# Attention with a gated MLP on one core: other costs for VectorE's queued side work, and none of it handed out in the last block of the MLP's first product

## The chip, the core and the metric

The kernel runs on one core of a Trainium2 chip. Its time is the device time of the whole program in microseconds (us). TensorE (PE in the profile) does the matmuls, VectorE (DVE) and ScalarE (ACT) the elementwise work, GpSimd (POOL) and SyncE (SP) issue DMA transfers from queues of their own. Each engine takes its instructions strictly in the order in which the program lists them.

## The reference

For x of 2048 rows by 1024 columns (bf16):

```
xn  = layernorm(x)
q, k, v = xn @ wqkv             (32 heads of 32 columns)
logits  = q . k[s - 2w], w = 0..7      (a window of 8, dilation 2; masked before row 0)
s   = (softmax(logits * scale) . v[s - 2w]) @ wo
g   = silu( (silu(xn @ w1) * (xn @ w3)) @ w2 )     (inner width 3584)
out = x + s * g
```

## The kernel before

The 2048 rows are worked in four chunks (0 to 3) of 512, one after the other. In each chunk TensorE runs, without a pause if it can:

- the projection to q, k and v (`qkv`, line 254): three times eight groups of eight matmuls of 128x128 by 128x512;
- the MLP's first product (`up_block`): 14 blocks (`fb` = 0 to 13), in each two pairs of groups, `g` from w1 and `u` from w3 (tile `gu`). ScalarE takes silu of `g` into `sg` (line 258), VectorE multiplies that by `u` into one of 28 tiles `ht` (line 260). That makes one `ht` per 16 matmuls;
- the MLP's second product (`down_half`, line 466), twice seven weight tiles, for the two halves of the columns. Each half has four accumulators `acc` in PSUM. All PSUM tiles of `gu` and `acc` come from one pool of six banks, so an accumulator waits until the last reader of its bank's tile before (an `sg` or an `ht`) is through;
- the output projection (`wo_proj`, line 421), in the middle of the second half, or in chunk 3 between the first half and the last (line 489).

The attention itself is done by VectorE beside this, as *side work*. An object `Side` holds a queue of items, each with a cost in us, a function that emits its instructions, and sometimes a gate, a time before which it may not go. `Side` has a clock of its own, counted at build time: after each piece of TensorE's work the program calls `side.step(dt, used)`. The clock goes on by `dt`; a credit grows by `dt − used`, up to 4.0; items are emitted from the head of the queue while the credit is positive, and each takes its cost off. So the costs decide at build time behind which `ht` an item stands on VectorE. They don't alter what an item does. A block of the first product steps twice by 2 * GRP, GRP being 1.727, with 0.7 used for the `ht`.

The items of a chunk, in order:

- eight Q·K windows: a product of 128x4096 (line 311), folds of 2048 and 1024 (line 322) and 512 (line 326) into `E`;
- `shuffle_out`: sixteen DMAs on POOL's queue move `E` to `L4` (line 342); the four loads of the next chunk's x (line 211) go to SP's queue;
- statistics and normalization of the next chunk (lines 199, 222, 231, 202; gate 12 us behind the shuffle; not in chunk 3). Four transposing DMAs on SP's queue (line 235) follow, one at the end of a block (`bring_one`), at the earliest 3 us of side clock after their `norm`;
- the softmax (gate 16 us behind the shuffle): three adds of `L4` into `z` (lines 364 to 366), maximum (369), subtraction (371), exp on ScalarE (358), sum (373), reciprocal (375), product `pb` (376). Silu, exp and the square root of line 225 each need a table load on ScalarE when the function changes;
- `shuffle_back`: sixteen DMAs on POOL's queue move `pb` to `Pr` (line 384);
- eight P·V products of 128x4096 (line 395, gate 16 us behind that shuffle) and seven joins (line 406) into `oT`, in the order product 0, product 1, join; then three times product, product, join, join.

`wo_proj` first flushes what is left in the queue; its matmuls read `oT`. SP's queue also carries the weight loads (line 136), two at a time in the second half of a block, and `load_wo` (line 193) after block 10. A weight load waits until TensorE is through with the tile whose place it takes.

Of the kernel before, what the change touches and what calls it, by code (L numbers as in the profile page):

```python
# [16 lines left out]
class Side:  # L17
# [7 lines left out]
    def add(self, cost, fn, gate=None):  # L25
        self.items.append((cost, fn, gate))

    def step(self, dt, used=0.0):
        self.now += dt
        self.credit = min(self.credit + dt - used, 4.0)  # L30
        while self.items and self.credit > 0:
            cost, fn, gate = self.items[0]
            if gate is not None and gate() > self.now:
                break
            self.items.popleft()
            fn()
            self.credit -= cost
# [8 lines left out]
def kernel(  # L46
# [11 lines left out]
    nc = tc.nc  # L58
    P = 128
    S, D, F = 2048, 1024, 3584  # L60
    Dh, W, DIL = 32, 8, 2
# [5 lines left out]
    FB = FT // 2  # L67
# [4 lines left out]
    GRP = 1.727  # L72
# [27 lines left out]
    side = Side()  # L100
# [53 lines left out]
    def load_x0(st):  # L154
# [15 lines left out]
        out=ident[:], in_=ident[:], compare_op=ALU.not_equal, fill=1.0,  # L170
# [9 lines left out]
        out=maskb[:], in_=maskb[:], compare_op=ALU.is_ge, fill=-1.0e9,  # L180
# [17 lines left out]
    def half_stats(x_t, stats, i):  # L198
        nc.vector.bn_stats(out=stats[:, i, :], in_=x_t[:, i * 512:(i + 1) * 512])  # L199

    def normalize(x_t, mean, rstd):
        nc.vector.tensor_scalar(
            out=x_t[:], in0=x_t[:], scalar1=mean, scalar2=rstd, op0=ALU.subtract, op1=ALU.mult,
        )

    def ln_side(c):
        xs = []
        for st in range(NST):
            x_t = xp.tile([P, D], BF16, tag="x")
            g = (c * NST + st) * P  # L210
            nc.sync.dma_start(out=x_t[:], in_=x_flat[g:g + P, :])
            xs.append(x_t)
        mv = small.tile([P, NST, nc.vector.BN_AGGR_DIM], FP32, tag="mv", bufs=2)
        rstd = small.tile([P, NST], FP32, tag="rstd", bufs=2)
        ready = side.now + 12.0
        mark = [0.0]

        def stat(st):
            stats = small.tile([P, 2, nc.vector.BN_STATS_DIM], FP32, tag="stats")
            half_stats(xs[st], stats, 0)  # L220
            half_stats(xs[st], stats, 1)
            nc.vector.bn_aggr(out=mv[:, st, :], in_=stats[:])

        def root():
            nc.scalar.activation(out=rstd[:], in_=mv[:, :, 1], func=ACTF.Sqrt, bias=eps_t[:], scale=1.0)
            mark[0] = side.now + 2.0

        for st in range(NST):
            side.add(1.45, lambda st=st: stat(st), lambda: ready)
        side.add(0.0, root)  # L230
        side.add(0.15, lambda: nc.vector.reciprocal(out=rstd[:], in_=rstd[:]), lambda: mark[0])
        nxt = xnT_pool.tile([P, KT, CH], BF16, tag="xnT", name="xnT_next")

        def bring(st):
            nc.sync.dma_start_transpose(out=nxt[:, :, st * P:(st + 1) * P], in_=xs[st][:])

        def norm(st):
            normalize(xs[st], mv[:, st, 0:1], rstd[:, st:st + 1])
            brings.append((side.now + 3.0, lambda: bring(st)))

        for st in range(NST):
            side.add(0.55, lambda st=st: norm(st))
        return nxt

    brings = deque()
# [17 lines left out]
    def up_block(c, xnT, fb):  # L263
        hts = []
        w1t, w3t = take_w(("1", fb)), take_w(("3", fb))
        for i in range(2):
            pss = []
            for wt in (w1t, w3t):
                ps = psum_mm.tile([P, CH], FP32, tag="mm", name=f"gu{c}_{fb}_{len(pss)}")
                mm_group(ps[:], lambda kt: wt[:, kt, i * P:(i + 1) * P], lambda kt: xnT[:, kt, :])  # L270
                pss.append(ps)
            if i == 1:
                load_w(2)
            hts.append(gate_up(*pss))
            side.step(2 * GRP, 0.7)
        bring_one()
        return hts

# [25 lines left out]
    att = {}  # L304

    def qk_side(c):
        E = block("E").rearrange("p (w s) -> p w s", w=W)

        def mul(w, prod):
            o = HALO - DIL * w  # L310
            nc.vector.tensor_mul(prod, qT[:], kT[:, :, o:o + CH])  # L311

        def one(w):
            hold = {}

            def first():
                hold["p"] = block("prod").rearrange("p (j s) -> p j s", j=NJ)
                mul(w, hold["p"])

            def fold(n):  # L320
                prod = hold["p"]
                nc.vector.tensor_add(prod[:, 0:n, :], prod[:, 0:n, :], prod[:, n:2 * n, :])  # L322

            def last():
                prod = hold["p"]
                nc.vector.tensor_add(E[:, w, :], prod[:, 0, :], prod[:, 1, :])  # L326

            side.add(2.2, first)
            side.add(1.15, lambda: fold(4))
            side.add(0.6, lambda: fold(2))  # L330
            side.add(0.35, last)

        for w in range(W):
            one(w)
        side.add(0.0, lambda: shuffle_out(c, E))
# [14 lines left out]
    def softmax_side(c, L4):  # L350
        z = sm.tile([P, W, P], FP32, tag="z")
        mx = sm.tile([P, P], FP32, tag="mx")
        ssum = mx
        pb = sm.tile([P, W, P], BF16, tag="pb")
        mark = [0.0]

        def expo():
            nc.scalar.activation(out=z[:], in_=z[:], func=ACTF.Exp, scale=scale)
            mark[0] = side.now + 3.4

        def mask():
            nc.vector.tensor_add(z[0:32, :, 0:HALO], z[0:32, :, 0:HALO], maskb[:])

        side.add(1.2, lambda: nc.vector.tensor_add(z[:], L4[:, 0], L4[:, 1]), lambda: att["L4_at"])
        side.add(1.2, lambda: nc.vector.tensor_add(z[:], z[:], L4[:, 2]))
        side.add(1.2, lambda: nc.vector.tensor_add(z[:], z[:], L4[:, 3]))
        if c == 0:
            side.add(0.3, mask)
        side.add(1.9, lambda: nc.vector.tensor_reduce(
            out=mx[:], in_=z[:].rearrange("p w s -> p s w"), axis=AX.X, op=ALU.max))  # L370
        side.add(1.2, lambda: nc.vector.tensor_sub(z[:], z[:], mx[:].unsqueeze(1).to_broadcast([P, W, P])))
        side.add(0.0, expo)
        side.add(1.9, lambda: nc.vector.tensor_reduce(
            out=ssum[:], in_=z[:].rearrange("p w s -> p s w"), axis=AX.X, op=ALU.add), lambda: mark[0])
        side.add(0.95, lambda: nc.vector.reciprocal(out=ssum[:], in_=ssum[:]))
        side.add(1.2, lambda: nc.vector.tensor_mul(pb[:], z[:], ssum[:].unsqueeze(1).to_broadcast([P, W, P])))  # L376
        side.add(0.0, lambda: shuffle_back(c, pb))

    def shuffle_back(c, pb):
# [9 lines left out]
    def pv_side(c, Pr, ready):  # L389
        oT = block("oT").rearrange("p (j s) -> p j s", j=NJ)  # L390
        att["oT"] = oT

        def pvmul(dst, w):
            o = HALO - DIL * w
            nc.vector.tensor_mul(  # L395
                dst, Pr[:, w, :].unsqueeze(1).to_broadcast([P, NJ, CH]), vT[:, :, o:o + CH]
            )

        hold = {}

        def part(key, w):
            hold[key] = block("pv").rearrange("p (j s) -> p j s", j=NJ)
            pvmul(hold[key], w)

        def join(a, b):
            nc.vector.tensor_add(a, a, b)  # L406

        side.add(2.2, lambda: pvmul(oT, 0), lambda: ready)
        side.add(2.2, lambda: part("B", 1))
        side.add(2.2, lambda: join(oT, hold["B"]))  # L410
        for w0 in (2, 4, 6):
            side.add(2.2, lambda w0=w0: part("B", w0))
            side.add(2.2, lambda w0=w0: part("C", w0 + 1))
            side.add(2.2, lambda: join(hold["B"], hold["C"]))
            side.add(2.2, lambda: join(oT, hold["B"]))

    def wo_piece(oT, was, st, c0, w):
        dh, n0 = divmod(c0, CH)
# [31 lines left out]
    def finish_half(c, dh, gts, s_sb, xres, queue):  # L450
        def one(st):
            finish(c, st, dh * 512, 512, gts[st][:], s_sb[:, st, dh * 512:(dh + 1) * 512], xres, queue)
        for st in range(NST):
            side.add(1.38, lambda st=st: one(st))

    def down_half(c, dh, hts, at):
        accs = [psum_mm.tile([P, 512], FP32, tag="mm", name=f"acc{c}_{dh}_{st}") for st in range(NST)]
# [104 lines left out]
    def copy_in(src, st, ks, eng):  # L562
# [28 lines left out]
        out=junk[:], in_=x0[1][:], func=ACTF.Square, bias=nm[:], scale=1.0 / 32.0, accum_out=mv0[1][:, 1:2],  # L591
# [17 lines left out]
    def part(kt, js, h):  # L609
        cs = slice(h * 256, (h + 1) * 256)  # L610
        for j in js:
            nc.tensor.matmul(  # L612
                qps[j][:, cs], lhsT=wq(kt, j), rhs=xcT[:, kt, cs],
                start=(kt == 0 and h == 0), stop=(kt == KT - 1), skip_group_check=True,
            )
# [106 lines left out]
```

## Time and profile before

| | |
|---|---|
| median of the runs | 821.23 us (820.35 to 821.45, 3 runs) |
| the profiled execution's own time | 820.01 us |
| its span, first to last instruction | 818.2 us |
| TensorE busy | 805.8 us (98%) |
| VectorE busy | 477.1 us (58%) |
| ScalarE busy | 181.5 us (22%) |
| POOL busy | 92.6 us (11%) |

In a row of the time line the first two numbers are the start and the length in us; then follow engine, line, operation, the tiles written and read and their shapes, how many of them are merged in the row, and in square brackets the engine's idle time ahead of it and what ended that. A row of the waits has the engine, tile and line that waited, what it waited for, and then the us in total, how often, and the longest. SPq and POOLq are the sequencers that issue DMAs. A DMA row without a start time names the transfer, its queue, the count and the median us from issue to landing. PE's ends are modelled, and a few per cent of its records are missing, so counts of matmuls in a row can be a few short.

### The profile page before, as it was taken

What the parts mean: (1) busy time and instruction counts of PE and PEld (TensorE: products, weight loads), DVE (VectorE), ACT (ScalarE), POOL (GpSimd) and SP (SyncE); (2) the same over time, 40 slices, a digit from 0 to 9 for tenths busy, and PEclk for the clock granted to TensorE, in tenths of its full rate; (3) what the DMA queues carried; (4) which work ended last, traced back from release to release, by engine and by line L of the source; (5) the groups of instructions that cost most, each with busy time, mean ns of one, the idle gap of its engine ahead of it and who ended that gap; (6) DMA issues with size and microseconds to landing.
All of it is one profiled execution on the core that took longest, in us unless ns stands there. A gap on an engine that the chain in (4) does not pass through costs nothing.

```text
span 818.2 us, 9453 instructions
## 1 busy us (share of the span) xinstructions
PE 805.8 (98%) x3742; PEld 406.8 (50%) x3816; DVE 477.1 (58%) x492; ACT 181.5 (22%) x293; POOL 92.6 (11%) x175
## 2 busy tenths in 40 slices
PE   9999999999999999999999999999999999999998
PEld 7654444444665444444466444444446644444443
DVE  6498564942239775792125958479311694639632
ACT  3031331012332133101133213210123311311120
POOL 0001321001100214000010031400000004030010
PEclk9999999999999999999999999999999999999999
DMA  9676999842366899964244799995434488687500
GB/s 299 185 196 199 206 189 275 255 152 78 109 199 164 222 194 224 277 222 144 76 161 118 205 216 205 203 301 186 138 94 150 110 210 186 165 242 221 179 31 22
DMA packets 195148, 147.44 MB, mean 180 GB/s; under 512 B 23584, under 2 KB 175904, under 8 KB 195104
## 3 DMA queue, kind: packets, MB, share of 16 engines
q1 hardware_dynamic: 189664, 134.76, 60.8%
q0 software_dynamic: 5440, 12.07, 6.7%
q8 instruction: 30, 0.49, 0.3%
q14 instruction: 14, 0.11, 0.1%
HBM read 130.02 MB, written 4.19 MB: 164 GB/s over the span
## 4 chain that ended last, share of the span: by engine, by line
PE 86%; DVE 7%; DMA 3%; issue 2%; POOL 1%; ACT 1%; DVEq 0%; ACTq 0%
PE gu L254 35%; PE acc L466 20%; PE ps_qkv L254 19%; PE ps_wo L421 7%; DMA Pr<-pb 3%; PE acc L489 3%; DVE pv L395 2%; PE ps_qkv L612 1%; POOL Pr L384 1%; DVE ht L260 1%; DVE oT L406 1%; DVE stats L199 1%; DVE pv L406 1%; ACT L258 0%; PE warm_ps L507 0%
## 5 line engine op out<-in xcount | busy, mean ns | idle before, releaser
L254 PE MATMUL gu<-xnT_next,w 128*128 128x512 bf16 x1317 | 289.5, 379 | 1.7 <-ACT sg L258 0.3
L254 PEld LDWEIGHTS <-w 128*128 128x128 bf16 x1792 | 175.3, 98 | 211.9 <-issue 0.9
L466 PE MATMUL acc<-w,ht 128*128 128x512 bf16 x767 | 169.6, 379 | 3.1 <-DVE ht L260 2.3
L254 PEld LDWEIGHTS <-wq 128*128 128x128 bf16 x720 | 103.2, 143 | 52.1
L260 DVE TENSOR_TENSOR ht<-sg,gu 128x512 bf16<-128x512 bf16 x112 | 75.9, 682 | 86.3 <-PE gu L254 65.1
L254 PE MATMUL ps_qkv<-xnT_next,wq 128*128 128x512 bf16 x565 | 124.2, 379 | 0.6
L466 PEld LDWEIGHTS <-ht 128*128 128x128 bf16 x784 | 76.6, 98 | 95.1 <-issue 2.9
L258 ACT ACTIVATE sg<-gu 128x512 bf16<-128x512 f32 x112 | 65.8, 597 | 261.4 <-PE gu L254 221.3
L311 DVE TENSOR_TENSOR prod<-qT,kT 128x4096 bf16<-128x4096 bf16 x32 | 73.1, 2286 | 68.5 <-ACT kT L282 68.5
L254 PE MATMUL gu<-xnT,w 128*128 128x512 bf16 x439 | 96.4, 379 | 0.5
L446 DVE TENSOR_TENSOR gt<-gt,s_sb 128x512 f32<-128x512 f32 x31 | 21.4, 690 | 122.2 <-ACT gt L440 68.5
L342 POOL DMA_DIRECT2D L<-E x64 | 37.1, 586 | 276.4 <-DVE E L326 264.1
L395 DVE TENSOR_TENSOR pv<-Pr,vT 128x4096 bf16<-128x4096 bf16 x28 | 63.3, 2287 | 0.0
L322 DVE TENSOR_TENSOR prod<-prod 128x2048 bf16<-128x2048 bf16 x64 | 61.2, 956 | 1.4
L421 PE MATMUL ps_wo<-wo,oT 128*128 128x512 bf16 (+2 forms) x260 | 55.9, 372 | 0.3
L440 ACT ACTIVATE gt<-acc 128x512 f32<-128x512 f32 x32 | 19.1, 597 | 149.6 <-PE acc L466 127.8
L448 POOL DMA_DIRECT2D out_dram<-o_t x28 | 15.3, 546 | 309.2 <-DVE o_t L447 309.2
L384 POOL DMA_DIRECT2D Pr<-pb x64 | 36.7, 579 | 108.1 <-DVE pb L376 98.0
L421 PEld LDWEIGHTS <-oT 128*128 128x128 bf16 x264 | 25.6, 98 | 30.0
L406 DVE TENSOR_TENSOR oT<-oT,pv 128x4096 bf16<-128x4096 bf16 x16 | 36.6, 2289 | 0.2
L433 ACT CAST s_sb<-ps_wo 128x512 bf16<-128x512 f32 x31 | 18.1, 585 | 66.4 <-PE ps_wo L421 66.4
L282 ACT CAST vT<-ps_qkv 128x512 bf16<-128x512 f32 x32 | 18.7, 585 | 59.7 <-PE ps_qkv L254 58.6
(81 smaller groups left out, 329.0 us busy)
## 6 DMA issues: line engine op xcount, KB each, us to landing
w<-in_B_w_dram SPq DMA_DIRECT2D x168, 512.0 KB, 5.4
wq<-in_A_wqkv_dram SPq DMA_DIRECT2D x44, 512.0 KB, 3.8
wo<-in_A_wo_dram SPq DMA_DIRECT2D x8, 1024.0 KB, 11.2
L<-E POOLq DMA_DIRECT2D x64, 64.0 KB, 7.0
Pr<-pb POOLq DMA_DIRECT2D x64, 64.0 KB, 5.4
xres<-in_A_x_dram SPq DMA_DIRECT2D x4, 1024.0 KB, 6.5
out_dram<-o_t POOLq DMA_DIRECT2D x28, 128.0 KB, 2.0
x_t<-in_A_x_dram SPq DMA_DIRECT2D x12, 256.0 KB, 6.2
```

Of the source, the lines that this page charges most:

```text
L254: nc.tensor.matmul(ps, lhsT=lhs(kt), rhs=rhs(kt), start=(kt == 0), stop=(kt == KT - 1))
L258: nc.scalar.activation(out=sg[:], in_=g_ps[:], func=ACTF.Silu)
L260: nc.vector.tensor_mul(ht[:], sg[:], u_ps[:])
L311: nc.vector.tensor_mul(prod, qT[:], kT[:, :, o:o + CH])
L322: nc.vector.tensor_add(prod[:, 0:n, :], prod[:, 0:n, :], prod[:, n:2 * n, :])
L342: nc.gpsimd.dma_start(out=L4[sq * NH:(sq + 1) * NH, r, :, :], in_=E_r[r, :, :, sq * P:(sq + 1) * P],)
L384: nc.gpsimd.dma_start(out=Pr_r[r, :, :, sq * P:(sq + 1) * P], in_=pb[sq * NH:(sq + 1) * NH, :, :],)
L395: nc.vector.tensor_mul(dst, Pr[:, w, :].unsqueeze(1).to_broadcast([P, NJ, CH]), vT[:, :, o:o + CH])
L406: nc.vector.tensor_add(a, a, b)
L421: nc.tensor.matmul(ps[:, 0:w], lhsT=oT[:, j, st * P:(st + 1) * P], rhs=was[dh][:, j, n0:n0 + w], start=(j == 0), stop=(j == NJ - 1),)
L466: nc.tensor.matmul(accs[st][:], lhsT=hts[f][:, st * P:(st + 1) * P], rhs=w2t[:, i, :], start=(f == 0), stop=(f == FT - 1),)
L489: nc.tensor.matmul(acc[:], lhsT=hts[f][:, st * P:(st + 1) * P], rhs=w2ts[f // 4][:, f % 4, :], start=(f == 0), stop=(f == FT - 1),)
```

## The change

`step` gets an argument `hold`: with it the clock and the credit go on, but no item is emitted. `up_block` sets it in the last of the 14 blocks and counts 0.72 for the `ht`. All costs of side items are set to other numbers. The functions that are emitted are the same.

```diff
-    def step(self, dt, used=0.0):
+    def step(self, dt, used=0.0, hold=False):
...
-        while self.items and self.credit > 0:
+        while not hold and self.items and self.credit > 0:
...
-            side.add(1.45, lambda st=st: stat(st), lambda: ready)
+            side.add(1.6, lambda st=st: stat(st), lambda: ready)
...
-        side.add(0.15, lambda: nc.vector.reciprocal(out=rstd[:], in_=rstd[:]), lambda: mark[0])
+        side.add(0.19, lambda: nc.vector.reciprocal(out=rstd[:], in_=rstd[:]), lambda: mark[0])
...
-            side.add(0.55, lambda st=st: norm(st))
+            side.add(0.57, lambda st=st: norm(st))
...
-            side.step(2 * GRP, 0.7)
+            side.step(2 * GRP, 0.72, hold=fb == FB - 1)
...
-            side.add(2.2, first)
-            side.add(1.15, lambda: fold(4))
-            side.add(0.6, lambda: fold(2))
-            side.add(0.35, last)
+            side.add(2.31, first)
+            side.add(1.25, lambda: fold(4))
+            side.add(0.71, lambda: fold(2))
+            side.add(0.45, last)
```

In the softmax 1.2 becomes 1.24 (three adds, subtraction, product `pb`), 1.9 becomes 1.93 (maximum, sum), 0.95 becomes 0.97 (reciprocal). All fifteen P·V products and joins go from 2.2 to 2.31, and the four last steps of a half's output (`finish_half`) from 1.38 to 1.44.

More of the change, by code (lines that the diff above doesn't have):

```diff
@@ L362, in mask @@
             nc.vector.tensor_add(z[0:32, :, 0:HALO], z[0:32, :, 0:HALO], maskb[:])
-        side.add(1.2, lambda: nc.vector.tensor_add(z[:], L4[:, 0], L4[:, 1]), lambda: att["L4_at"])
-        side.add(1.2, lambda: nc.vector.tensor_add(z[:], z[:], L4[:, 2]))
-        side.add(1.2, lambda: nc.vector.tensor_add(z[:], z[:], L4[:, 3]))
+        side.add(1.24, lambda: nc.vector.tensor_add(z[:], L4[:, 0], L4[:, 1]), lambda: att["L4_at"])
+        side.add(1.24, lambda: nc.vector.tensor_add(z[:], z[:], L4[:, 2]))
+        side.add(1.24, lambda: nc.vector.tensor_add(z[:], z[:], L4[:, 3]))
         if c == 0:
             side.add(0.3, mask)
-        side.add(1.9, lambda: nc.vector.tensor_reduce(
+        side.add(1.93, lambda: nc.vector.tensor_reduce(
             out=mx[:], in_=z[:].rearrange("p w s -> p s w"), axis=AX.X, op=ALU.max))
-        side.add(1.2, lambda: nc.vector.tensor_sub(z[:], z[:], mx[:].unsqueeze(1).to_broadcast([P, W, P])))
+        side.add(1.24, lambda: nc.vector.tensor_sub(z[:], z[:], mx[:].unsqueeze(1).to_broadcast([P, W, P])))
         side.add(0.0, expo)
-        side.add(1.9, lambda: nc.vector.tensor_reduce(
+        side.add(1.93, lambda: nc.vector.tensor_reduce(
             out=ssum[:], in_=z[:].rearrange("p w s -> p s w"), axis=AX.X, op=ALU.add), lambda: mark[0])
-        side.add(0.95, lambda: nc.vector.reciprocal(out=ssum[:], in_=ssum[:]))
-        side.add(1.2, lambda: nc.vector.tensor_mul(pb[:], z[:], ssum[:].unsqueeze(1).to_broadcast([P, W, P])))
+        side.add(0.97, lambda: nc.vector.reciprocal(out=ssum[:], in_=ssum[:]))
+        side.add(1.24, lambda: nc.vector.tensor_mul(pb[:], z[:], ssum[:].unsqueeze(1).to_broadcast([P, W, P])))
         side.add(0.0, lambda: shuffle_back(c, pb))
@@ L406, in join @@
             nc.vector.tensor_add(a, a, b)
-        side.add(2.2, lambda: pvmul(oT, 0), lambda: ready)
-        side.add(2.2, lambda: part("B", 1))
-        side.add(2.2, lambda: join(oT, hold["B"]))
+        side.add(2.31, lambda: pvmul(oT, 0), lambda: ready)
+        side.add(2.31, lambda: part("B", 1))
+        side.add(2.31, lambda: join(oT, hold["B"]))
         for w0 in (2, 4, 6):
[L412 to L415, printed above, removed]
+            side.add(2.31, lambda w0=w0: part("B", w0))
+            side.add(2.31, lambda w0=w0: part("C", w0 + 1))
+            side.add(2.31, lambda: join(hold["B"], hold["C"]))
+            side.add(2.31, lambda: join(oT, hold["B"]))
     def wo_piece(oT, was, st, c0, w):
@@ L453, in finish_half @@
         for st in range(NST):
-            side.add(1.38, lambda st=st: one(st))
+            side.add(1.44, lambda st=st: one(st))
     def down_half(c, dh, hts, at):
```

## The prediction

> **What bounds the kernel now.** I read the page first, then the waits by engine, then the time line around each of TensorE's waits. TensorE is busy for 98% of the span, so the change can only move the time through the gaps in TensorE's row.
>
> ```profile
> PE 805.8 (98%) x3742; PEld 406.8 (50%) x3816; DVE 477.1 (58%) x492; ACT 181.5 (22%) x293; POOL 92.6 (11%) x175
> PE acc L466 <- DVE ht L260: 2.3, 3, 1.1
> PE gu L254 <- ACT sg L258: 0.3, 1, 0.3
> ```
>
> Apart from the start (the warm-up and the first transposes, which the change doesn't touch), TensorE waits four times: three times for an `ht` of VectorE, 2.3 us, once for an `sg` of ScalarE, 0.3 us. The time line puts them at three places:
>
> ```profile
> 548.71 0.81 PE L466 MATMUL acc<-w,ht 128*128 128x512 bf16 x3
> 549.78 1.89 PE L466 MATMUL acc<-w,ht 128*128 128x512 bf16 x8 [0.27 <-DVE ht L260]
> 552.59 32.10 PE L466 MATMUL acc<-w,ht 128*128 128x512 bf16 x145 [0.91 <-DVE ht L260]
> ...
> 750.70 2.75 PE L466 MATMUL acc<-w,ht 128*128 128x512 bf16 x12
> 754.56 21.74 PE L466 MATMUL acc<-w,ht 128*128 128x512 bf16 x98 [1.11 <-DVE ht L260]
> ...
> 709.26 7.07 PE L254 MATMUL gu<-xnT_next,w 128*128 128x512 bf16 x31 [0.25 <-ACT sg L258]
> ```
>
> Two lie where the MLP's second product begins, in chunk 2 (1.18 us) and chunk 3 (1.11 us). What VectorE did there in chunk 2:
>
> ```profile
> 528.06 0.69 DVE L260 TENSOR_TENSOR ht<-sg,gu 128x512 bf16<-128x512 bf16 x1 [2.76 <-remote]
> 536.84 2.29 DVE L395 TENSOR_TENSOR oT<-Pr,vT 128x4096 bf16<-128x4096 bf16 x1 [8.09 <-DMA Pr<-pb]
> 539.05 2.29 DVE L395 TENSOR_TENSOR pv<-Pr,vT 128x4096 bf16<-128x4096 bf16 x1
> 541.25 0.68 DVE L260 TENSOR_TENSOR ht<-sg,gu 128x512 bf16<-128x512 bf16 x1
> ...
> 549.05 0.68 DVE L260 TENSOR_TENSOR ht<-sg,gu 128x512 bf16<-128x512 bf16 x1
> ...
> 551.85 0.68 DVE L260 TENSOR_TENSOR ht<-sg,gu 128x512 bf16<-128x512 bf16 x1
> ```
>
> I number the 28 `ht` of a chunk 0 to 27. `ht`21 is the one at 528.06. The first P·V product is queued right behind it and waits 8.09 us for the shuffled probabilities (`Pr`); `ht`22 and `ht`23, whose inputs are long there, are stuck behind. `ht`24 ends at 549.73 and `ht`25 at 552.53, which is where TensorE's two gaps end (549.78, 552.59). So the second and the fourth accumulator of the product take the PSUM banks that `ht`24 and `ht`25 read last; the waits in the built program name the same two in both kernels. `ht`26 and `ht`27 hold no early bank.
>
> **The change part by part.**
>
> *The costs.* They decide behind which `ht` an item is queued; its work stays the same. A Q·K window takes 645.25 − 640.60 = 4.65 us here, priced 4.30 before and 4.72 after:
>
> ```profile
> 640.60 2.29 DVE L311 TENSOR_TENSOR prod<-qT,kT 128x4096 bf16<-128x4096 bf16 x1 [22.12 <-ACT kT L282]
> 645.25 2.29 DVE L311 TENSOR_TENSOR prod<-qT,kT 128x4096 bf16<-128x4096 bf16 x1
> ```
>
> Eight windows are priced 8 × 0.42 = 3.36 us more, about one step of the side clock (2 × 1.727 = 3.454 us, one `ht`). In the built order the first shuffle moves from behind `ht`6 to behind `ht`7, the statistics from `ht`10 to `ht`11, and `pb` from behind `ht`15 to `ht`17 in chunks 1 and 2, from `ht`16 to `ht`17 in chunk 0 and from `ht`14 to `ht`15 in chunk 3. The first P·V product goes from `ht`21 to `ht`23 in chunks 1 and 2, from 22 to 23 in chunk 0, from 19 to 21 in chunk 3.
>
> How late does `pb` become? In chunk 2:
>
> ```profile
> 490.68 1.28 DVE L199 BATCH_NORM_STATS2 stats<-x_t 128x6 f32<-128x512 bf16 x2
> 508.56 1.22 DVE L371 TENSOR_TENSOR z<-z,mx 128x1024 f32<-128x1024 f32 x1
> 512.81 0.69 DVE L260 TENSOR_TENSOR ht<-sg,gu 128x512 bf16<-128x512 bf16 x1 [3.03 <-ACT sg L258]
> 516.34 1.23 DVE L376 TENSOR_TENSOR pb<-z,mx 128x1024 bf16<-128x1024 f32 x1
> ```
>
> From the statistics to the end of the subtraction (509.78) VectorE works or waits for ScalarE's table loads; it does the same work after, with as many `ht` between, one step later: 513.23. Then exp, a table load and an `sg` stand before the next `ht` (3.03 us), and 4.76 us from that `ht` to the end of `pb` (517.57). Both stay. So `pb` ends one step later, not two: 521.0. `Pr` was usable 19.27 us after `pb`; the first P·V moves from 536.84 to 540.3. `ht`22 and `ht`23 are now ahead of it and done by 535.7 (undisturbed `ht` come every 3.45 us from 528.06). Behind it the order is: two products, `ht`24, a join, `ht`25. A product or join costs 2.21 us of spacing (539.05 − 536.84), an `ht` 0.60. `ht`24 ends at 540.3 + 4.4 + 0.7 = 545.4, `ht`25 at 540.3 + 4.4 + 0.6 + 2.2 + 0.7 = 548.2. TensorE needs them four and twelve matmuls after 548.71, at 0.216 us each (sixteen in the 3.45 us of an undisturbed `ht`): 549.6 and 551.3. Both gaps go, with 4.2 and 3.1 us to spare. Bounds: one step later is my value; nothing later would only add slack; two full steps (the plan's own move) put `ht`25 at 551.6, a gap of 0.3. Chunks 0 and 1 have the same order after:
>
> ```profile
> 135.78 2.29 DVE L395 TENSOR_TENSOR oT<-Pr,vT 128x4096 bf16<-128x4096 bf16 x1 [4.16 <-DMA Pr<-pb]
> 147.92 12.25 PE L466 MATMUL acc<-w,ht 128*128 128x512 bf16 x55
> 333.51 2.29 DVE L395 TENSOR_TENSOR oT<-Pr,vT 128x4096 bf16<-128x4096 bf16 x1 [5.06 <-DMA Pr<-pb]
> 348.22 34.70 PE L466 MATMUL acc<-w,ht 128*128 128x512 bf16 x157
> ```
>
> One step gives `ht`25 at 147.1 against 150.5, and 344.9 against 350.8: no new gap, 3.4 and 5.9 us to spare.
>
> *Chunk 3* has no layer norm to prepare, so the shuffle of the logits sets its pace:
>
> ```profile
> 681.49 0.69 DVE L260 TENSOR_TENSOR ht<-sg,gu 128x512 bf16<-128x512 bf16 x1 [0.18 <-PE gu L254]
> 698.79 1.23 DVE L364 TENSOR_TENSOR z<-L 128x1024 f32<-128x1024 bf16 x1 [2.80 <-DMA L<-E]
> 704.99 1.22 DVE L371 TENSOR_TENSOR z<-z,mx 128x1024 f32<-128x1024 f32 x1
> 709.24 0.69 DVE L260 TENSOR_TENSOR ht<-sg,gu 128x512 bf16<-128x512 bf16 x1 [3.03 <-ACT sg L258]
> 713.20 1.21 DVE L376 TENSOR_TENSOR pb<-z,mx 128x1024 bf16<-128x1024 f32 x1
> ...
> 731.01 2.29 DVE L395 TENSOR_TENSOR oT<-Pr,vT 128x4096 bf16<-128x4096 bf16 x1 [6.99 <-DMA Pr<-pb]
> 753.82 0.69 DVE L260 TENSOR_TENSOR ht<-sg,gu 128x512 bf16<-128x512 bf16 x1
> ```
>
> Three folds more come behind `ht`7, so the last `E` and with it `z` come some 3 us later (701.8). `pb` ends at about 717.1 (714.41 before), `Pr` at 733.7. `ht`25 stood behind nine products and joins and six `ht` and ended at 754.51; after, six and four: 733.7 + 13.2 + 2.4 + 0.1 = 749.4, needed by 750.70 − 0.25 + 2.6 = 753.0. That gap goes, 3.6 us to spare. The 0.25 us at 709.26: the exp and its two table loads held an `sg` until 708.6, 8 us behind its place; after, they stand two `sg` later and hold one until 711.7, 4 us behind. It goes too.
>
> *The hold.* No item goes out around `ht`26 and `ht`27, for whose banks nobody waits early; by itself worth 0. Its cost: the work runs later into the second product. Latest in chunk 3, where the output projection flushes the queue and needs `oT`. Eight products and joins are left behind `ht`27; before, four took 9.15 us:
>
> ```profile
> 760.02 4.50 DVE L395 TENSOR_TENSOR pv<-Pr,vT 128x4096 bf16<-128x4096 bf16 x2
> 766.88 2.29 DVE L406 TENSOR_TENSOR oT<-oT,pv 128x4096 bf16<-128x4096 bf16 x1
> 776.14 12.25 PE L421 MATMUL ps_wo<-wo,oT 128*128 128x512 bf16 x55
> ```
>
> 752.6 + 18.3 = 770.9, needed at about 776.1 − 1.4 = 774.7: 3.8 us to spare. If that cover is gone, each us costs one.
>
> *SP and POOL.* The four `x_t` loads move behind one more pair of weight loads, the transposes one block (6.9 us) later, `wo` behind the fourth of them. Consumers: statistics at 494.1 for loads issued near 480, the next chunk's projection and the output projection tens of us on. The weight loads behind them wait for TensorE anyway. Cost 0; POOL keeps its order.
>
> ```profile
> 473.15 2.30 SPq L211 DMA_DIRECT2D x_t<-in_A_x_dram  x4
> 477.91 22.90 SPq L136 DMA_DIRECT2D w<-in_B_w_dram  x8
> 321.24 2.56 SPq L235 DMA_TRANSPOSE xnT_next<-x_t  x1
> 521.54 1.65 SPq L235 DMA_TRANSPOSE xnT_next<-x_t  x1
> xnT_next<-x_t SPq DMA_TRANSPOSE x12, 6.5
> ```
>
> **Sum.** 2.3 + 0.3 = 2.6 us off the profiled execution's 820.01 (span 818.2, 1.8 around it): 817.4. The median shown is 821.23, 1.2 above that execution, so 818.6. The measurement tells about 0.2% (1.64 us) from no change.
>
> **Rivals.**
> *A: the gaps partly return* (chance 0.22). `Pr` needed 16.25 to 19.27 us from `pb` in the four chunks. If it comes 4 us later than I reckon everywhere, 0.6, 0.9 and 0.4 us of gap stand in chunks 0, 2 and 3: gain 0.7, 820.5, no change. For it: the slack of 3 to 4 us is one spread of that shuffle. Against: three chunks must be late at once to lose most.
> *B: slower* (0.05). The fourth transpose (521.54) starts inside the shuffle of `Pr` in chunks 0 to 2 and the third does so too after. If a transpose held the POOL rows back for its whole 6.5 us (its median to landing), `ht`25 would be late by 3.1 in chunk 0, 0.6 in chunk 1 and 3.4 in chunk 2: 7.1 − 2.6 = 4.5 us slower, 825.7. It decides from 4.6 us of delay per chunk, where chunks 0 and 2 together give back the 2.6. Against: chunk 1 had one inside (321.24) and took 16.25 us, chunk 3 had none and took 16.60. The Trainium skill, "DMA: Bandwidth & Descriptors", Queues, rings and completion order, says that each DMA engine takes turns between queues packet by packet; by that rule the rows share with the transpose instead of queuing behind it, which speaks for a smaller delay than B's.
> *C: it doesn't do what it says* (0.05): the gaps wait for another `ht` than I read. If the fourth accumulator needed `ht`26, two products behind `ht`25, that ends at 553.2 in chunk 2 and 152.1 in chunk 0, 1.9 and 1.6 us late: 3.5 − 2.6 = 0.9 us slower, 822.1, still no change. Against: the ends 549.73 and 552.53 fit `ht`24 and `ht`25 alone.
>
> **Chances.** Forecast 0.68, A 0.22, B 0.05, C 0.05: faster 0.68, same 0.27, slower 0.05. The range reaches from 0.8 us under the forecast (the runs shown spread by 1.1) to 820.9, past A.
>
> **What would show it.** Right: no wait of `acc` L466 for `ht` and none of `gu` for `sg`; the idle time before the first P·V in chunk 2 near 4.6 us in place of 8.09, its start near 540 on the old clock; the last join of chunk 3 some 4 us before `ps_wo`. Wrong: `acc` still waits, a wait of `ps_wo` for `oT`, or `Pr` more than 22 us behind `pb`.

## The result and the profile after

The changed kernel took 817.01 us (median of 5 runs, 816.60 to 818.11) beside 821.19 us of the kernel before (5 runs, 819.92 to 821.45): a ratio of 0.9955, 95% interval 0.9941 to 0.9970. The forecast was faster by 2.6 us, to 818.6; the time lies below the range, which began at 817.8. The profiled execution took 816.60 us, with a span of 814.7.

First two lines of the page of the changed kernel (busy time and share by engine; each engine's share of the chain of work that ended last), then its waits of TensorE, all three of them, then two pieces of that chain (start, length, work): the start of the matmuls of line 254, and the last group of eight of line 421 that the chain runs through.

```profile
PE 808.9 (99%) x3816; PEld 406.6 (50%) x3816; DVE 479.6 (59%) x492; ACT 181.8 (22%) x293; POOL 92.7 (11%) x175
PE 99%; DVE 0%; issue 0%; DVEq 0%
```

```profile
PE warm_ps L507 <- DVE warm L164: 1.2, 1, 1.2
PE ps_qkv L612 <- DVE xcT L563: 0.5, 1, 0.5
PE xt L551 <- DVE dg L538: 0.3, 1, 0.3
```

```profile
20.09 31.08 PE ps_qkv L254 x144
...
809.17 1.31 PE ps_wo L421 x8
```

What is left are waits of the start. No `acc` waits for an `ht` and no `gu` for an `sg`. From 20.09 to 809.17, 789.08 us, TensorE doesn't stop once. The same two pieces of the kernel before:

```profile
20.31 0.22 PE ps_qkv L254
...
812.57 1.31 PE ps_wo L421 x8
```

That is 792.26 us, so its gaps were worth 3.17 us (the unrounded starts give the last digit). Of the rest of the difference, 0.22 us lies in the start. (The chain shows a matmul from the end of the one before it, 0.16 us behind its own start; the start of line 254 itself is at 19.93 us after and 20.15 before.) The time line of VectorE in chunk 2, after:

```profile
534.74 0.69 DVE L260 TENSOR_TENSOR ht<-sg,gu 128x512 bf16<-128x512 bf16 x1 [2.77 <-PE gu L254]
541.77 2.29 DVE L395 TENSOR_TENSOR oT<-Pr,vT 128x4096 bf16<-128x4096 bf16 x1 [6.34 <-DMA Pr<-pb]
543.98 2.28 DVE L395 TENSOR_TENSOR pv<-Pr,vT 128x4096 bf16<-128x4096 bf16 x1
546.18 0.68 DVE L260 TENSOR_TENSOR ht<-sg,gu 128x512 bf16<-128x512 bf16 x1
546.78 2.28 DVE L406 TENSOR_TENSOR oT<-oT,pv 128x4096 bf16<-128x4096 bf16 x1
548.98 0.68 DVE L260 TENSOR_TENSOR ht<-sg,gu 128x512 bf16<-128x512 bf16 x1
```

`ht`23 runs at 534.74, undisturbed, ahead of the wait for `Pr`. `ht`24 ends at 546.86 and `ht`25 at 549.66. TensorE started the second product at 548.28 without a pause:

```profile
546.77 1.67 PE L254 MATMUL gu<-xnT_next,w 128*128 128x512 bf16 x7
548.28 7.93 PE L466 MATMUL acc<-w,ht 128*128 128x512 bf16 x36
```

VectorE still stands idle for 6.34 us. What changed is that `ht`23 no longer stands behind that wait, and that the `ht` that do, `ht`24 and `ht`25, are through before TensorE needs their banks.

### The profile page after: what moved, and what is told of

Same layout as the page of the kernel before. It is cut to its first block, busy times and chain, and to the rows that moved or that the text cites. A ratio compares the mean times of both kernels' runs of the same rounds, so it can differ in the third digit from the quotient of the medians.

```text
span 814.7 us, 9515 instructions
## 1 busy us (share of the span) xinstructions
PE 808.9 (99%) x3816; PEld 406.6 (50%) x3816; DVE 479.6 (59%) x492; ACT 181.8 (22%) x293; POOL 92.7 (11%) x175
## 4 chain that ended last, share of the span: by engine, by line
PE 99%; DVE 0%; issue 0%; DVEq 0%
PE gu L254 47%; PE acc L466 21%; PE ps_qkv L254 19%; PE ps_wo L421 7%; PE acc L489 3%; PE ps_qkv L612 1%; PE warm_ps L507 0%; DVE xcT L563 0%; PE xt L545 0%; PE tp L559 0%; PE xt L551 0%; DVE gt L446 0%; PE r_ps L636 0%; DVE o_t L447 0%; DVE warm L164 0%
## 5 line engine op out<-in xcount | busy, mean ns | idle before, releaser
L466 PE MATMUL acc<-w,ht 128*128 128x512 bf16 x784 | 170.4, 379 | 0.0
L466 PEld LDWEIGHTS <-ht 128*128 128x128 bf16 x784 | 76.7, 98 | 92.5
```

Of the source, the lines that this page charges most:

```text
L466: nc.tensor.matmul(accs[st][:], lhsT=hts[f][:, st * P:(st + 1) * P], rhs=w2t[:, i, :], start=(f == 0), stop=(f == FT - 1),)
```

## The experiments

Theory O: the order does it. With the first P·V product queued behind `ht`23, the two `ht` that hold the first PSUM banks of the second product are no longer late. Rival H: the hold does it, by keeping the last block free. Later came theory S, on the size: the gaps of the kernel before vary from one execution to the next with its shuffles, and the changed kernel has slack (time by which `ht`25 ends ahead of TensorE's need of its bank) that swallows this. In the tables below, "gaps" is the time from the start of the first matmul of line 254 to that last group of eight of line 421, less 789.08 us, in the profiled execution. Ratios are to the kernel before, run beside each.

### The parts alone

**e1**: the new costs, without the hold.

```diff
-            side.step(2 * GRP, 0.72, hold=fb == FB - 1)
+            side.step(2 * GRP, 0.72)
```

> The new costs without the hold. Theory O (the order: the first P.V product is queued behind a later ht, so ht24 and ht25 no longer stand behind its wait) expects the whole gain: 817.0, no wait of acc for ht. Rival H (the hold frees the last block of the first product and so the start of the second) expects the waits of acc for ht to stay and 820 to 821.

**e2**: the kernel before with the hold alone.

```diff
-            side.step(2 * GRP, 0.7)
+            side.step(2 * GRP, 0.7, hold=fb == FB - 1)
```

> The hold with the old costs. Theory O expects no change from the kernel before, 820 to 821.2, with about 2.3 us of acc waiting for ht in chunks 2 and 3, since nobody waits early for ht26 and ht27. Rival H expects 817 to 818 and no such wait.

**e3**: the kernel before with one number changed.

```diff
-        pv_side(c, Pr, side.now + 16.0)
+        pv_side(c, Pr, side.now + 23.0)
```

> The kernel before with one number changed: the gate of the P.V products 23 us behind their shuffle in place of 16, so that the first P.V product stands behind ht23 (chunks 1, 2) as in the changed kernel, with all costs old and no hold. Theory O expects the waits of acc for ht to be gone and the wait of gu for sg in chunk 3 (0.25 us shown) to stay: 817.4. Rival H, and a rival by which the costs matter through the spacing of the P.V items, expect 820 to 821.

**e4**: the changed kernel without the hold and with the old costs of the Q·K windows (2.2, 1.15, 0.6, 0.35).

> The new costs of everything but the Q.K windows, no hold. The shuffle of the logits stays behind ht6, but the first P.V product still goes to a later ht through the softmax costs. Theory O expects 817 to 817.5 with at most 0.2 us of acc waiting in chunk 2. A rival by which the move of the shuffle by the Q.K costs carries the gain expects 820 to 821.

| kernel | median us (runs) | ratio to before, 95% | gaps us |
|---|---|---|---|
| before, beside these | 819.08 (35) | | |
| e1 new costs, no hold | 817.11 (12) | 0.9980, 0.9971 to 0.9988 | 0.00 |
| e2 hold alone | 819.42 (11) | 1.0004, 0.9995 to 1.0013 | 1.83 |
| e3 gate 23 alone | 817.14 (11) | 0.9980, 0.9971 to 0.9988 | 0.00 |
| e4 new costs but Q·K, no hold | 817.09 (11) | 0.9978, 0.9969 to 0.9986 | 0.01 |

H falls on both sides: without the hold the whole gain is there, and the hold alone brings nothing. (e2 lies below the 820 to 821.2 expected of it because the kernel before, too, stood lower beside it than in the first runs.) The time lines of e2, VectorE's and then TensorE's, show why. No side item stands between its last two `ht` (555.17, two in one row), but TensorE's gap ends at 553.10, on the `ht` before them:

```profile
537.36 2.29 DVE L395 TENSOR_TENSOR oT<-Pr,vT 128x4096 bf16<-128x4096 bf16 x1 [7.85 <-DMA Pr<-pb]
...
552.37 0.68 DVE L260 TENSOR_TENSOR ht<-sg,gu 128x512 bf16<-128x512 bf16 x1
552.97 2.29 DVE L406 TENSOR_TENSOR oT<-oT,pv 128x4096 bf16<-128x4096 bf16 x1
555.17 1.28 DVE L260 TENSOR_TENSOR ht<-sg,gu 128x512 bf16<-128x512 bf16 x2
```

```profile
549.27 2.92 PE L466 MATMUL acc<-w,ht 128*128 128x512 bf16 x12
553.10 7.07 PE L466 MATMUL acc<-w,ht 128*128 128x512 bf16 x32 [0.91 <-DVE ht L260]
```

e3 is the cleanest support of O: no cost is touched and only the place of the P·V work moves. Its time line of VectorE in chunk 2, with `ht`23 ahead of the first product:

```profile
535.27 0.69 DVE L260 TENSOR_TENSOR ht<-sg,gu 128x512 bf16<-128x512 bf16 x1 [2.76 <-PE gu L254]
536.96 2.29 DVE L395 TENSOR_TENSOR oT<-Pr,vT 128x4096 bf16<-128x4096 bf16 x1 [1.01 <-DMA Pr<-pb]
```

In one point e3 missed: the wait of `gu` for `sg` in chunk 3 had been expected to stay, and it is gone in this execution. `z` began 16.64 us behind the last `E` in chunk 3 of e3, 17.48 in the first profile; so that wait hangs on when the first shuffle lands. The kernel before bears this out: in its five traced executions `z` came 17.48, 16.89, 17.25, 17.47 and 17.23 us behind `E`, and TensorE paused there for 0.41, 0, 0.19, 0.41 and 0.15 us by the starts of its matmuls.

### The order turned the other way

**e7**: the changed kernel with the gate at 9 in place of 16, which queues P·V two `ht` earlier.

```diff
-        pv_side(c, Pr, side.now + 16.0)
+        pv_side(c, Pr, side.now + 9.0)
```

> The changed kernel with the gate of the P.V products 9 us behind their shuffle in place of 16: costs new, hold in place, but the first P.V product queued two ht earlier, so that it waits longer with more ht behind it. Theory O expects much more waiting than before the change: gaps in chunks 0, 2 and 3 and 6 to 13 us on the changed kernel, 823 to 830. Rival H expects no more than the time before, 821.

**e8**: the kernel before with the new costs of the Q·K windows alone (2.31, 1.25, 0.71, 0.45).

> The kernel before with the new costs of the Q.K windows alone. The first shuffle and pb come one ht later, the first P.V product behind ht22 in chunk 2. Theory O expects the gap of chunk 3 gone and 1 to 2 us of acc waiting for ht24 and ht25 in chunk 2 left: 818.5 to 820. The rival by which the Q.K costs carry the gain expects 817.

e7 took 835.35 us (4 runs), ratio 1.0198 (1.0178 to 1.0219), with gaps of 18.10: hold and new costs both in place, and yet far slower than either kernel. The direction is that of O. The size is beyond its range, because TensorE now waits inside the first product too, ahead of the accumulators; and the gaps lie in chunks 0, 1 and 2, not in 3 as expected. The waits of e7:

```profile
PE gu L254 <- DVE ht L260: 9.0, 3, 4.7
PE acc L466 <- DVE ht L260: 4.5, 5, 1.6
```

e8 took 825.61 us (4 runs), ratio 1.0096 (1.0068 to 1.0124), where 818.5 to 820 had been expected. Its gaps, 5.83 us in the profiled execution, lie in chunks 0, 1 and 2, but for a short wait of `gu` for `sg` (0.2 us shown) in chunk 3. In chunk 1 (VectorE, then TensorE) `Pr` comes 19.61 us behind `pb` in place of 16.25, and the first product stands behind one `ht` fewer than in the changed kernel:

```profile
332.22 0.69 DVE L260 TENSOR_TENSOR ht<-sg,gu 128x512 bf16<-128x512 bf16 x1 [2.77 <-PE gu L254]
341.33 2.29 DVE L395 TENSOR_TENSOR oT<-Pr,vT 128x4096 bf16<-128x4096 bf16 x1 [8.43 <-DMA Pr<-pb]
```

```profile
351.48 1.89 PE L466 MATMUL acc<-w,ht 128*128 128x512 bf16 x8 [1.24 <-DVE ht L260]
354.28 31.89 PE L466 MATMUL acc<-w,ht 128*128 128x512 bf16 x144 [0.91 <-DVE ht L260]
```

In chunk 0 the first product stands behind `ht`23, as in the changed kernel, and yet TensorE waits for `ht`25. With the old prices of the P·V items two of them, a join and a product, stand between `ht`24 and `ht`25; in the changed kernel it is the join alone. VectorE's rows from `ht`24 to `ht`25, then TensorE's:

```profile
145.78 0.68 DVE L260 TENSOR_TENSOR ht<-sg,gu 128x512 bf16<-128x512 bf16 x1
146.37 2.28 DVE L406 TENSOR_TENSOR oT<-oT,pv 128x4096 bf16<-128x4096 bf16 x1
148.58 2.29 DVE L395 TENSOR_TENSOR pv<-Pr,vT 128x4096 bf16<-128x4096 bf16 x1
150.78 0.68 DVE L260 TENSOR_TENSOR ht<-sg,gu 128x512 bf16<-128x512 bf16 x1
```

```profile
151.51 31.89 PE L466 MATMUL acc<-w,ht 128*128 128x512 bf16 x145 [0.67 <-DVE ht L260]
```

So setting the Q·K costs close to their measured lengths (4.72 for a window of 4.65 us), alone, makes this kernel slower: truer numbers are worth nothing in themselves. What counts is which `ht` the P·V work lands behind, how many of its items stand between `ht`24 and `ht`25, and when the second shuffle lands.

### The size: does the kernel before vary by its gaps?

**e5, e6, e14, e15**: four more executions of the kernel before. **e9**: the changed kernel again.

> The kernel before, another profiled execution. If the gaps follow the shuffle of the probabilities (theory O with a shuffle that varies), an execution near 821.2 shows longer waits of acc for ht than 2.3 us, about as much longer as it is slower than 820.0, behind a later start of the first P.V product. If the waits stay at 2.3 us and the time differs, the rest lies outside the gaps, at the start or the end.

> The same once more: a third execution of the kernel before, for the spread of the shuffle and of the gaps.

> A fourth profiled execution of the kernel before. Theory S: its span is the start of the second projection's matmuls, plus 789.08 us, plus the gaps, plus 5.74 us, so an execution that is slower than 820.2 has gaps of over 3.2 us and one near 817.5 has under 1 us.

> A fifth execution of the kernel before. Theory S expects the same sum: start of the second projection's matmuls + 789.08 + gaps + 5.74 us gives the span, and the gaps are longer where Pr and L come later behind pb and the last E.

> The changed kernel once more, beside many runs of the kernel before. If the gaps of the kernel before vary from run to run (theory S, spread) and the changed kernel has none, the changed kernel stands at 817.0 to 817.2 with a small spread, and the gain is what the kernel before happens to lose: about 2.0 us beside a median of 819.1. If the first measurement's 4.2 us belongs to the change itself, the changed kernel stands at about 815.

| execution | time us | start of line 254 | gaps | 789.08 + 5.74 + both | span |
|---|---|---|---|---|---|
| before, first profile | 820.01 | 20.15 | 3.17 | 818.14 | 818.15 |
| before, e5 | 819.99 | 20.45 | 2.85 | 818.12 | 818.13 |
| before, e6 | 820.18 | 20.86 | 2.64 | 818.32 | 818.33 |
| before, e14 | 819.51 | 20.53 | 2.30 | 817.65 | 817.66 |
| before, e15 | 818.91 | 20.70 | 1.53 | 817.05 | 817.05 |
| after, first profile | 816.60 | 19.93 | 0.01 | 814.76 | 814.74 |
| after, e9 | 817.17 | 20.31 | 0.17 | 815.30 | 815.31 |

The sum accounts for every span to 0.02 us: the executions of the kernel before differ in the start (0.7 us between the extremes) and in the gaps (1.53 to 3.17), and in nothing else. By its definition the column of gaps is what is left over between the start and the end. Counted singly instead, as pauses between the starts of TensorE's matmuls, with each missing record (74 in a trace, none in the first one after) taken as one place of 0.216 us, the gaps come to 3.18, 2.86, 2.65, 2.31 and 1.53 us for the five executions of the kernel before, and to 0 and 0.17 for the two after: the same to 0.02 us. The waits of `acc` in e14 and e15, against 2.3 us in the first profile:

```profile
PE acc L466 <- DVE ht L260: 1.3, 3, 0.9
```

```profile
PE acc L466 <- DVE ht L260: 1.1, 2, 0.6
```

In e15 the first P·V product of chunk 2 began at 536.54 after 7.25 us of waiting, with a start 0.55 us later than in the first profile (536.84, 8.09): `Pr` came 18.43 us behind `pb` in place of 19.27. e9 had a median of 817.28 us (12 runs) beside 818.96 of the kernel before (28 runs), ratio 0.9980 (0.9971 to 0.9989). So the changed kernel stands where it stood, and the gain is what the kernel before happens to lose. The 0.17 us of e9 is one pause in chunk 2, at 551.43: `Pr` came 22.30 us behind `pb` there, and `ht`25 was through 0.1 us too late. So the changed kernel stands close to the edge in that chunk.

**e10, e11**: both kernels with a delay ahead of the second shuffle, two in-place copies of 1.04 us each on POOL that change no value.

```diff
+        for _ in range(2):
+            nc.gpsimd.tensor_copy(out=pb[:], in_=pb[:])
         Pr = block("Pr").rearrange("p (w s) -> p w s", w=W)
```

> The kernel before, with two in-place copies of pb on POOL ahead of the second shuffle, so that Pr comes about 2 us later; nothing is computed differently. Theory S expects the delay more than once in the end: about 819 + 2 per chunk where ht25 is late (chunks 2 and 3) plus part of 2 in chunks 0 and 1, 823 to 826. A rival by which the run-to-run spread has another source expects less than 1 us more.

> The changed kernel with the same two copies ahead of the second shuffle. Its ht25 ended 1.2 us (chunk 2), 1.6 us (chunk 1) and more (chunks 0, 3) ahead of need in the profile, so 2 us later cost 0 to 2 us: 817 to 819. If the slack isn't what takes the delay, it costs as much as in the kernel before.

The kernel before went to 823.58 us (4 runs; ratio 1.0053, 1.0037 to 1.0068), its gaps to 5.80. The changed kernel went to 818.58 (10 runs, 816.72 to 819.97; ratio 0.9993, 0.9983 to 1.0003), with gaps of 0.29 in the profiled execution, a run of 817.55. So the two copies cost the one 4.6 us (823.58 − 818.96) and the other 1.3 (818.58 − 817.28). They didn't make `Pr` 2.1 us later everywhere. Against the first profile of the same kernel it came 1.2, 3.0, 1.0 and 0.2 us later behind `pb` in e10 (chunks 0 to 3), and 1.3, −0.9, 0.5 and 5.5 us in e11. So the runs show that the changed kernel bears such a disturbance far better, not how much it bears in each chunk; for that chunk 3 of e11 is the one measure, where `Pr` 5.5 us later cost TensorE a pause of 0.29 us, all of that execution's gaps. TensorE in chunk 2 of e10 (two lines have been added, so L468 is L466): a wait of `gu` comes before the two known ones.

```profile
549.75 1.89 PE L254 MATMUL gu<-xnT_next,w 128*128 128x512 bf16 x8 [1.04 <-DVE ht L260]
551.48 0.81 PE L468 MATMUL acc<-w,ht 128*128 128x512 bf16 x3
552.55 1.89 PE L468 MATMUL acc<-w,ht 128*128 128x512 bf16 x8 [0.27 <-DVE ht L260]
555.36 6.85 PE L468 MATMUL acc<-w,ht 128*128 128x512 bf16 x31 [0.91 <-DVE ht L260]
```

### Why the second shuffle takes longer after

In the changed kernel `Pr` came 18.78, 20.59, 20.95 and 14.45 us behind `pb` (chunks 0 to 3), before 18.49, 16.25, 19.27 and 16.60.

**e12**: `wo` loaded behind block 13 (`if fb == 10` becomes `if fb == 13`).

> The changed kernel with the two loads of wo issued after block 13 in place of block 10. If these 2 MB are what made the second shuffle 4 us longer in chunk 1 of the changed kernel (20.6 us against 16.25 before), Pr comes 16 to 18 us behind pb in chunks 1 and 2. If the transposes beside it did that, it stays at 20 to 21 us. The time stays at 817.1 either way, since nothing waits.

**e13**: the transposes sent behind the last block.

```diff
-            brings.append((side.now + 3.0, lambda: bring(st)))
+            brings.append((side.now + 60.0, lambda: bring(st)))
```

> The changed kernel with all four transposes of a chunk sent to SP's queue only behind the last block of the first product, so that none runs beside the second shuffle. Rival B's mechanism (a transpose beside the shuffle lengthens it) expects Pr 16 to 18 us behind pb in chunks 1 and 2, against 20.6 and 21.0 in the changed kernel. If the transposes don't matter, it stays at 19.5 to 21. The time stays at 817.0 to 817.4 either way.

e12: 18.13, 19.88, 21.33, 15.20, time 817.39 (10 runs): `wo` isn't it. e13: 15.45, 16.52, 16.29, 14.65, time 817.00 (10 runs): the transposes are. Each is one execution, but the drop is beyond the spread: with the transposes in their place (after, e1, e9, e12) it was 18.1 to 19.7, 18.9 to 20.7 and 20.9 to 22.3 us in chunks 0 to 2, and chunk 3, which has no transposes, was at 13.9 to 15.2. The queue of SP in the changed kernel in chunk 2, where the shuffle runs from 520.8 to 541.8, shows two of them beside it:

```profile
521.31 1.39 SPq L235 DMA_TRANSPOSE xnT_next<-x_t  x1
526.03 2.10 SPq L136 DMA_DIRECT2D w<-in_B_w_dram  x2
528.22 1.50 SPq L235 DMA_TRANSPOSE xnT_next<-x_t  x1
529.77 4.95 SPq L193 DMA_DIRECT2D wo<-in_A_wo_dram  x2
```

and VectorE in chunk 2 of e13 how much sooner `Pr` is there:

```profile
535.14 0.69 DVE L260 TENSOR_TENSOR ht<-sg,gu 128x512 bf16<-128x512 bf16 x1 [2.77 <-PE gu L254]
537.48 2.29 DVE L395 TENSOR_TENSOR oT<-Pr,vT 128x4096 bf16<-128x4096 bf16 x1 [1.65 <-DMA Pr<-pb]
```

The time doesn't move, since neither kernel has gaps; but the slack of chunk 2 grows from 1.2 to 5.9 us. No version tried was faster than the changed kernel by more than its spread: with no gap left, the order of the side work has nothing more to give.

## Why the prediction was right and wrong, point by point

- **What bounds the kernel** (the gaps alone): right. The span is a constant, the start and the gaps.
- **Which `ht` hold the banks, and that rival C is out**: right. The gaps are gone though `ht`26 ends 6.4 us behind the start of the second product in chunk 2 (554.66 against 548.28), about as late as before (6.6).
- **The hold is worth 0**: right (e1, e2).
- **`pb` one step later**: right in chunks 0 to 2. It ends at 520.81 in chunk 2, 3.24 us later by a clock that starts 0.23 us earlier. In chunk 3 the adds of `L` waited a second time (1.98 us), and `pb`, at 716.98, was 1.6 us later than reckoned (TensorE came into that chunk 1.7 us earlier than before, so this is 718.7 on the old clock, where 717.1 had been forecast), while the shuffle was 2.15 us shorter than before; the two errors nearly cancelled, by luck.
- **`Pr` 19.27 us behind `pb` in chunk 2**: too short, 20.95, and in chunk 1 20.59 in place of 16.25. The slack was 1.2 us in chunk 2, not 3.1, and the idle time ahead of the first product 6.34 us, not 4.6; in e9 `Pr` passed even the 22 us that the prediction gave as a sign of being wrong, at a price of 0.17 us. That is rival B's mechanism: the prediction held against it that chunk 1 had a transpose inside its shuffle and took 16.25 us, but after the change two run beside it from issue to landing. e13 puts their cost together at 3.3, 4.1 and 4.7 us in chunks 0 to 2, less than B's 6.5 for one. This agrees in direction with the rule cited there (the Trainium skill, "DMA: Bandwidth & Descriptors", Queues, rings and completion order: a DMA engine takes turns between queues by packet): in chunk 2 the two transposes took 7.1 and 11.0 us from issue to landing, and the shuffle grew by only 4.7. Why the kernel before took 16.25 us in chunk 1 and 19.27 in chunk 2, with one whole transpose and the end of another beside the shuffle in both, the runs don't show.
- **The wait for `sg` goes**: it did, but its absence shows little. It comes and goes in the kernel before too, and in the first profile after `z` came 17.05 us behind `E` in chunk 3, sooner than in every execution of the kernel before that paused there (17.23 the least). e4 is better evidence: `z` 17.57 us behind, and no pause.
- **The flush has cover**: right. The last join of chunk 3 ended at 768.64, `ps_wo` started at 772.75: 4.1 us to spare, 3.8 forecast.
- **The sum**: here it failed, in two terms, while the mechanism held. The first, "2.3 + 0.3 = 2.6 us", was 3.17. A matmul is shown as 379 ns long while the next follows after 216, so the last one ahead of a gap covers 0.16 us of it, and there were four gaps: 2.5 + 4 × 0.16 = 3.2. The second, "The median shown is 821.23, 1.2 above that execution, so 818.6", carried 1.2 us of the kernel before's surplus over to the changed kernel. In the traced executions of the kernel before (818.91 to 820.18 us) such differences are gaps of 1.53 to 3.17 us and 0.7 us of start, and the changed kernel has no such gaps (0 and 0.17). From the profiled execution itself, 820.01 − 3.17 = 816.84; measured 817.01. The range went down only 0.8 us from 818.6 and so began above both.
- **Against the median of before** the gain was 4.2 us on the first runs, and for the changed kernel again 1.7 us beside 28 later runs (e9; median of before 818.96). Two other kernels without gaps gained 2.0 and 2.7 us beside 35 and 13 runs (e1, e13; 819.08 and 819.68). The forecast 2.6 lies among these, in part by luck: the profile that it was read from had the longest gaps of the five traced (their mean is 2.50), and reading them 0.57 us too short offset that. Why the first five runs of the kernel before (819.92 to 821.45) were higher than most later ones is open: by the sum, 821.2 us needs gaps of about 4 us, and e10, with `Pr` later by 0.2 to 3.0 us in the four chunks, has 5.80, but no trace of such an execution is at hand. The later sets come from three chips (medians of the kernel before 818.63 to 819.68), and which chip the first runs were on isn't on record, so a difference between chips isn't ruled out.

## What to carry to other kernels

Beside a saturated engine, ask of every queued side item which instruction of the main path stands behind it and what that one holds: here, in chunk 2, a wait of VectorE for a DMA is harmless behind `ht`23 (6.3 us) and holds TensorE up behind `ht`21 (8.1 us). Where a change removes waits altogether, forecast from what is left when they are zero, and not by a difference from a median that contains them; the waits here varied from run to run, and their variation went with them. Measure a gap between the starts of matmuls, not by the idle time shown, and mind that a missing record looks like a pause of 0.216 us.

## What the runs showed of the hardware

- Two DMA transposes beside sixteen transfers of 64 KB on another queue made the sixteen together 3.3 to 4.7 us longer (e13 against the changed kernel, one execution each). Moving the 2 MB of `wo` loads away from them made no difference that can be seen (e12).
- The start varied between 19.93 and 20.91 us over the profiled executions (the latter in e2), with its instructions unchanged.
- In the stretch without gaps TensorE took 789.08 or 789.09 us in six kernels (after, e1, e3, e4, e12, e13): a floor that is repeatable to 0.01 us.
